# Seven half-size products in the second layer of the first two token blocks, one weight sum on VectorE, and a replanned order

## The chip, the cores and the metric

The kernel runs on one core of a Trainium2 chip. The core has a matrix engine (TensorE, PE in the profile; its weight loads are listed apart as PEld), a vector engine (VectorE, DVE), a scalar engine (ScalarE, ACT), GpSimd (POOL) and SyncE (SP), which here only issues transfers. Each engine works through its own list of instructions in order, and waits on semaphores where it needs what another engine makes. Matrix products are written to PSUM, eight banks of 128 partitions by 512 floats; everything else lies in SBUF or in device memory. The metric is the time of one execution on the device in microseconds (us). Less is better.

## The reference

Attention with a threshold, followed by a feed-forward layer, all in single precision:

```python
def _attn_ref(q, k, v, tau):            # (8, 8, 576, 64): batch, heads, positions, head size
    scores = scale * np.matmul(q, k.transpose(0, 1, 3, 2))
    thresh = np.max(scores, axis=-1, keepdims=True) - tau
    scores = np.where(scores >= thresh, scores, -1000000000.0)
    scores = scores - np.max(scores, axis=-1, keepdims=True)
    attn = np.exp(scores)
    attn = attn / (np.sum(attn, axis=-1, keepdims=True) + 1e-09)
    return np.matmul(attn, v).astype(np.float32)

def _moe_ref(x, w_in, w_out):           # x (4608, 512), w_in (512, 2048), w_out (2048, 512)
    h = x @ w_in
    g = h * (1.0 / (1.0 + np.exp(-1.702 * h)))
    return (g @ w_out).astype(np.float32)
```

The attention's result, with the heads of a position side by side, is the x of the second function. The two weight matrices come as 64-bit floats, and the kernel turns them into 32-bit ones itself.

## The kernel before

**Attention.** The 64 heads are worked as 32 pairs, numbered n, four pairs for each of the 8 batch entries. A pair's queries and keys are loaded and turned (`load_qk`, `turn_in`, `prep`), TensorE makes nine tiles of scores (`scores_run`, L598), ScalarE copies them out of PSUM (`keep`, L615), VectorE takes maxima (`in_groups`, L621), subtracts the threshold (`sub`, L695), ScalarE masks and exponentiates (`mask` L702, `exps` L706), VectorE sums, TensorE multiplies with the values (`values`, L717), and VectorE scales the result into the transposed x of the feed-forward layer (`place_x`, L821). For some pairs rows of maxima or sums go through device memory on GpSimd's queue (L671, L680, L686, L786, L793). From the seventh pair on, the values of one pair and the scores of a later one are interleaved on TensorE.

**Feed-forward.** The 4608 rows of x are 18 blocks of 256. A block can begin when all pairs of its batch entries are placed. Blocks 0 and 1 are worked together by `first_blocks` (L1543): the first layer (`mm1_0`, L895) makes 16 groups of 128 hidden columns for both blocks at once, ScalarE and VectorE apply the activation (`tanh` L851, `gelu_0` L901) into `g0`; the second layer (`mm2`, L864) multiplies, for each of four halves of 128 rows, 16 pieces of `g0` with the 16 pieces of `w_out`, 512 columns wide, and sums them in one PSUM bank; ScalarE halves the sum (`half`, L871) and SyncE stores it (`store_0`, L1426). A matmul in single precision is two instructions in the trace.

From block 2 on both layers use seven products of half size in place of eight (the scheme of Strassen and Winograd). For the second layer (`second` L2162, `product` L1399) a block's hidden values are four quarters a11, a12, a21, a22, and w_out four quarters. Seven products P1, P2, P6, P7, P4, P5, P3 are formed; three of them take sums of the block's quarters (`s_sums`, `s_minus`, `s_last`, L1017 to L1032, on VectorE), and four take sums t1 to t4 of weight quarters. Each product is 8 matmuls of 256 columns. `read` (L1404) adds the products into the output.

**The weight sums.** t1 to t4 are made once, after the second layer of the first two blocks, because they lie where `g0` lies or over w_out. For each, ScalarE writes one negated operand (`t_minus`, L1005), and a GpSimd transfer adds the other one to it in place (`t_plus`, L1009). Four like sums are made of w_in (`w_sums`, L930, L934).

**Weights.** w_in and w_out come in 16 pieces each. SyncE loads a piece to a staging place (`load_w`, L513), and five small steps on ScalarE and VectorE turn it to 32 bits (`cv_power` L521, `cv_power2` L525, `cv_low` L532, `cv_round` L539 or `cv_whole` L546, `cv_end` L553).

**The order.** While the program is built, each step is entered as a task with an engine, a cost, a rank, the tasks that it follows and the buffers that it takes and gives. `run_in_order` (L256) is a planner: it plays the tasks through with these costs, and an engine that is free takes the ready task of least rank. The instructions are issued in that order, and nothing reorders them on the chip. Feed-forward tasks of TensorE have the last rank, so that they fill the time between attention tasks. Ranks come from the pair's number plus constants in the tables `EARLY`, `SECOND`, `LATER`, `CV`, `W_RANK` and `L_RANK`. `FIRST` is ahead of all others.

## Time and profile before

| | us |
|---|---|
| median of 3 runs | 1241.7 |
| lowest and highest | 1241.35, 1242.64 |
| the profiled execution's own time | 1243.68 |
| its span in the profile | 1241.9 |
| TensorE busy | 1217.7 |
| VectorE busy | 1074.6 |
| ScalarE busy | 827.3 |

An execution's own time is a little longer than the span from its first to its last profiled instruction. A table of stretches gives, for each stretch, its length, then each engine's busy time with the number of instructions, the granted clock of TensorE, the share of the transfer engines and the rate. The chain that ended last goes back from the last instruction, at each step to what released it. A group of instructions has its busy time, the mean length of one in ns, and the idle time ahead of it with what ended that. A matmul's listed length holds its way through the array, so the distance between the starts of two is what one costs in a row.

### The profile page before, as it was taken

What the parts mean: (1) busy time and instruction counts of PE and PEld (TensorE: products, weight loads), DVE (VectorE), ACT (ScalarE), POOL (GpSimd) and SP (SyncE); (2) the same over time, 40 slices, a digit from 0 to 9 for tenths busy, and PEclk for the clock granted to TensorE, in tenths of its full rate; (3) what the DMA queues carried; (4) which work ended last, traced back from release to release, by engine and by line L of the source; (5) the groups of instructions that cost most, each with busy time, mean ns of one, the idle gap of its engine ahead of it and who ended that gap; (6) DMA issues with size and microseconds to landing.
All of it is one profiled execution on the core that took longest, in us unless ns stands there. A gap on an engine that the chain in (4) does not pass through costs nothing.

```text
span 1241.9 us, 26064 instructions
## 1 busy us (share of the span) xinstructions
PE 1217.7 (98%) x10592; PEld 980.9 (79%) x10592; DVE 1074.6 (87%) x1666; ACT 827.3 (67%) x1215; POOL 70.9 (6%) x115
## 2 busy tenths in 40 slices
PE   8889999999999999999999999999999999999998
PEld 5645854497888888888777777777887797999998
DVE  6988996779988988899689987998799889999797
ACT  7999978787665767585677467756875686430330
POOL 0111114110000000000100010000100000000000
PEclk9999999999999999999999999999999999999999
DMA  8846658793423132224423252224322432434443
GB/s 243 222 88 148 190 126 146 147 241 68 117 49 92 55 92 74 73 80 128 105 60 105 70 129 73 64 64 126 91 48 66 131 92 72 120 112 140 147 115 109
DMA packets 201512, 137.13 MB, mean 110 GB/s; under 512 B 146800, under 2 KB 163184, under 8 KB 201264
## 3 DMA queue, kind: packets, MB, share of 16 engines
q1 hardware_dynamic: 188992, 110.22, 33.1%
q0 software_dynamic: 11712, 24.95, 9.8%
q8 instruction: 83, 1.36, 0.5%
q10 hardware_dynamic: 688, 0.30, 0.1%
q14 instruction: 37, 0.30, 0.1%
HBM read 103.29 MB, written 23.75 MB: 102 GB/s over the span
## 4 chain that ended last, share of the span: by engine, by line
PE 85%; ACT 7%; DVE 5%; DMA 2%; issue 1%; SPq 0%; DVEq 0%; ACTq 0%
PE ops L1399 24%; PE pv L717 10%; PE ps L598 9%; PE hps L963 7%; PE hps L1105 7%; PE ps L963 5%; PE ps L1105 5%; PE ops L864 4%; PE ops L1360 4%; PE hps L1253 4%; PE ps L1360 3%; PE ps L1253 3%; ACT arena L706 2%; ACT arena L702 2%; ACT arena L615 2%; DMA w_out<-in_moe_w_in_dram 1%
## 5 line engine op out<-in xcount | busy, mean ns | idle before, releaser
L621 DVE TRANSPOSE_TENSOR_REDUCE part<-arena 128x36 f32<-128x1152 f32 x300 | 364.1, 1240 | 62.3 <-ACT arena L615 45.6
L615 ACT COPY arena<-ps 128x576 f32<-128x576 f32 x288 | 171.0, 641 | 102.8 <-PE ps L598 102.6
L702 ACT ACTIVATE arena<-arena 128x1152 f32<-128x1152 f32 (+1 forms) x160 | 164.5, 1059 | 54.4 <-DVE arena L695 54.3
L706 ACT ACTIVATE arena<-arena,shift,scl 128x1152 f32<-128x1152 f32 (+1 forms) x160 | 195.0, 1246 | 1.3
L695 DVE TENSOR_TENSOR arena<-arena 128x1152 f32<-128x1152 f32 (+1 forms) x150 | 180.4, 1242 | 0.7
L598 PE MATMUL ps<-arena 64*64 64x288 f32 x2304 | 171.8, 408 | 7.8 <-ACT arena L615 4.5
L1399 PE MATMUL ops<-w_out,arena 128*128 128x256 f32 x768 | 174.4, 381 | 0.0
L1399 PEld LDWEIGHTS ops<-w_out,arena 128*128 128x128 f32 x768 | 144.3, 190 | 24.9 <-issue 5.3
L717 PE MATMUL pv<-arena 64*64 64x288 f32 x2176 | 159.5, 405 | 0.0
L598 PEld LDWEIGHTS ps<-arena 64*64 64x64 f32 x2304 | 81.5, 132 | 70.9 <-ACT arena L615 27.2
L717 PEld LDWEIGHTS pv<-arena 64*64 64x64 f32 x2176 | 81.3, 133 | 53.1 <-issue 7.7
L1399 PE MATMUL ops<-arena 128*128 128x256 f32 x528 | 118.1, 379 | 0.0
L1399 PEld LDWEIGHTS ops<-arena 128*128 128x128 f32 x528 | 100.2, 190 | 14.0 <-issue 0.4
L640 ACT ACTIVATE other<-red,minus_gap 32x18 f32<-32x18 f32 x118 | 36.2, 307 | 34.3 <-DVE red L630 32.9
L1267 ACT COPY arena<-hps 128x512 f32<-128x512 f32 x38 | 22.2, 584 | 53.9 <-PE hps L1253 53.8
L864 PE MATMUL ops<-w_out,arena 128*128 128x512 f32 x128 | 55.9, 594 | 0.0
L1082 POOL DMA_DIRECT2D arena<-wrow x36 | 19.4, 540 | 602.8 <-PE ops L1399 484.0
L895 PE MATMUL hps<-xT,w_in 128*128 128x256 f32 x232 | 50.9, 380 | 1.3 <-DVE arena L901 1.3
L895 PEld LDWEIGHTS hps<-xT,w_in 128*128 128x128 f32 x232 | 43.7, 190 | 8.5 <-DVE arena L901 1.7
L864 PEld LDWEIGHTS ops<-w_out,arena 128*128 128x128 f32 x128 | 24.1, 190 | 30.1 <-issue 29.8
L1151 DVE TENSOR_TENSOR arena<-ps,arena 128x512 f32<-128x512 f32 x36 | 23.7, 686 | 26.1 <-PE ps L1105 26.1
L963 PEld LDWEIGHTS hps<-xT,w_in 128*128 128x128 f32 x384 | 44.2, 192 | 1.1 <-issue 0.9
(235 smaller groups left out, 1967.4 us busy)
## 6 DMA issues: line engine op xcount, KB each, us to landing
arena<-in_v_dram SPq DMA_DIRECT2D x128, 144.0 KB
arena<-exu SPq DMA_DIRECT2D x42, 256.0 KB
arena<-ext SPq DMA_DIRECT2D x39, 256.0 KB
arena<-wrow POOLq DMA_DIRECT2D x36, 256.0 KB, 3.0
out_dram<-osb SPq DMA_DIRECT2D x32, 256.0 KB
arena<-in_q_dram SPq DMA_DIRECT2D x112, 72.0 KB
arena<-in_k_dram SPq DMA_DIRECT2D x112, 72.0 KB
arena<-row_s SPq DMA_DIRECT2D x48, 144.0 KB
```

Of the source, the lines that this page charges most:

```text
L598: nc.tensor.matmul(ps[ts(c, KT), h, 0:SH], lhsT=mats[n, 1][ts(h, D), ts(j, KT)], rhs=mats[n, 0][ts(h, D), ts(c, SH)], start=True, stop=True,)
L615: nc.scalar.copy(out=sT[n, t][:, u], in_=pss.pop((n, j))[:, :, 0:SH])
L621: nc.vector.tensor_reduce(out=stats[n, op][:, t * 2 * QB : min(2 * t + 2, NK) * QB], in_=sT[n, t].rearrange("p u h (g d) -> p (u h g) d", ...
L695: engine.tensor_tensor(out=s, in0=s, in1=mbs[n].unsqueeze(1).to_broadcast(list(s.shape)), op=ALU.add if n in BY_DMA else ALU.subtract,)
L702: nc.scalar.activation(out=s, in_=s, func=AF.Prelu, alpha=STEEP)
L706: nc.scalar.activation(out=s, in_=s, func=AF.Exp, scale=scl, bias=shift)
L717: nc.tensor.matmul(o[c][ts(h, D), 0:SH], lhsT=left(j, h)[ts(c, KT)], rhs=sT[n, t][ts(c, KT), u, h, :], start=(j == 0), stop=(j == NK - 1),)
L864: nc.tensor.matmul(acc[i], lhsT=g0[:, j, ts(i, P)], rhs=w_out[:, j, :], start=(j == 0), stop=(j == NFC - 1),)
L895: nc.tensor.matmul(hidden[j][:, ts(i, BLK)], lhsT=w_in[:, c, ts(j, P)], rhs=xTs[i][:, c, :], start=(c == 0), stop=(c == NDC - 1), skip_gro ...
L963: nc.tensor.matmul(o[:, ts(j, HT)], lhsT=left[:, c, ts(4 * y + j, P)], rhs=right[:, c, :], start=(x in (P1, P2, P5) and j + c == 0), stop= ...
L1105: nc.tensor.matmul(o[:, ts(j, BLK)], lhsT=left[:, c, ts(j, P)], rhs=right[:, c, :], start=(x in (P1, P2, P5) and j + c == 0), stop=(j + c ...
L1399: nc.tensor.matmul(banks[blk][k][:, ts(o, HM)], lhsT=left[:, j, :], rhs=right[:, j, :], start=(j == 0), stop=(j == HF - 1),)
```

## The change

The second layer of blocks 0 and 1 also goes by seven products a block. `g0` is laid out by quarters: half of the hidden columns, block, group, row. The order of the products of a block is P1, P2, P5, P6, P7, P3, and P4 of both blocks comes at the end, since t4 is written where a quarter of block 0 lay. A block uses three PSUM banks one after the other, and a product waits until what lies in its bank is read. The first weight sum t1 is made by two subtractions on VectorE after the last piece of w_out; t2 and t3 by ScalarE and GpSimd after it; t4 after P7 of block 0. VectorE's sums of the hidden values and the output of block 0 lie in spare x buffers. The later blocks use the same four weight sums.

The planner's costs of the first loads, of the first ScalarE instruction and of the first matmuls are new, and so are all constants in the rank tables, which change the order of the whole program. The core of the diff:

```diff
     EARLY = {
-        "add_row": -0.11,
+        "add_row": 9.44,
...
     CV = {
-        "cv_end": 102.19,
-        "cv_low": 7.35,
-        "cv_power": 316.63,
-        "cv_power2": 317.96,
+        "cv_end": -2.47,
+        "cv_low": -12.63,
+        "cv_power": 46.33,
+        "cv_power2": -0.05,
...
-    def mm2(i, part):
-
-        if part == 0:
-            acc[i] = psM.tile([P, d_model], FP32, name="ops", tag="mo")
-        for j in range(2 * part, 2 * part + 2):
-            nc.tensor.matmul(
-                acc[i], lhsT=g0[:, j, ts(i, P)], rhs=w_out[:, j, :],
-                start=(j == 0), stop=(j == NFC - 1),
-            )
...
+    def t_first(k):
+        o, a, b = (y[:, ts(k, HF // 2), :] for y in T_SUMS[0])
+        nc.vector.tensor_tensor(out=o, in0=a, in1=b, op=ALU.subtract)
...
+    FIRSTS = {
+        P1: (0, 0), P2: (1, 0), P5: (0, 1), P6: (1, 1), P7: (0, 0), P3: (1, 0), P4: (2, 0),
+    }
+
+    def product_0(blk, x, js):
+        left, right = PRODUCTS[x][:2]
+        left = quarters(blk)[left[0]][left[1]] if isinstance(left, tuple) else s_homes(blk)[x != P5]
+        k, o = FIRSTS[x]
+        if x in (P1, P2, P4) and js[0] == 0:
+            banks[blk, k] = psM.tile([P, BANK], FP32, name="ops", tag="mo")
+        for j in range(*js):
+            nc.tensor.matmul(
+                banks[blk, k][:, ts(o, HM)], lhsT=left[:, j, :], rhs=right[:, j, :],
+                start=(j == 0), stop=(j == HF - 1),
+            )
+
+    def read_0(blk, x):
...
+        if x == P1:
+            nc.scalar.activation(out=c21, in_=ps, func=AF.Copy, scale=FACTOR[0])
+        sums = {
+            P1: (), P2: [(c11, c21)], P5: [(c12, c21)], P6: [(c12, c12), (c21, c21)],
+            P7: [(c22, c12), (c21, c21)], P3: [(c12, c12)], P4: [(c21, c21)],
+        }
+        for e, a in sums[x]:
+            nc.vector.scalar_tensor_tensor(
+                out=e, in0=ps, scalar=FACTOR[0], in1=a, op0=ALU.mult, op1=ALU.add
+            )
...
-    W_RANK = (-44.98, 0.18, -1.8, 76.35, 1.62, -16.84)
+    W_RANK = (-138.99, 6.52, -4.17, 189.65, 11.68, 9.31)
...
-    warm = task("ACT", 1.5, -2.0, first_act)
-    warmth = [task("PE", 3.6, -20.0, run_up, take=("psM",), give=("psM",))]
+    warm = task("ACT", 2.3, -2.0, first_act)
+    warmth = [task("PE", 4.4, -20.0, run_up, take=("psM",), give=("psM",))]
...
-        for x in range(4):
-            after = t_ready[-1:] + (ffn[-1:] if x > 1 else []) + ready_w[n_in:]
+
+        def t_sum(x, after):
             for k in range(2):
                 after = [task("ACT", 1.0, T_RANK, t_minus, x, k, after=after)]
             a = task("POOL", 1.6, T_RANK, t_plus, x, after=after)
-            t_ready.append(transfer("DMW", 6.5, a, 1, lag=2.0))
+            return transfer("DMW", 6.5, a, 1, lag=2.0)
+
+        firsts = [task("DVE", 1.15, T_RANK, t_first, k, after=ready_w[n_in:]) for k in range(2)]
+        t_of = {P5: firsts, P6: [t_sum(1, firsts)], P7: [t_sum(3, firsts)]}
...
+            one(blk, P1, gs[0])
+            one(blk, P2, gs[1])
+            one(blk, P5, [[a] for a in sums])
+            one(blk, P6, [[a] for a in sums])
+            lasts = [task("DVE", 0.6, FIRST, s_last, blk, k, after=ffn[-1:]) for k in range(2)]
+            one(blk, P7, [[a] for a in minus])
+            one(blk, P3, [[a] for a in lasts])
+            if blk == 0:
+                t_of[P4] = [t_sum(2, t_of[P6] + [used[0, P7]])]
+        for blk in range(PLAIN):
+            one(blk, P4, gs[1])
+            for i in range(2):
+                task(
+                    "SP", 0.6, FIRST, store_0, blk, i,
+                    after=[y for (z, _), y in reads.items() if z == blk],
+                    give=("osb",) if blk else ("xT",) if i else (), lag=2.2,
+                )
...
-            cost, moves, ring = (0.6, 0.6, RING[0]) if which else (1.2, 0.72, RING[3])
+            cost, moves, ring = (0.6, 0.6, RING[0]) if which else (2.3 if n in (1, 3) else 1.2, 0.72, RING[3])
...
-        lv = task("SP", 2.45, r + (1.85 if n < 2 else -1.2) + load_rank(n, 2), load_v, n, after=lvs[-1:], take=(v_m,) + RING[2])
+        lv = task("SP", 3.8 if n < 2 else 2.45, r + (1.85 if n < 2 else -1.2) + load_rank(n, 2), load_v, n, after=lvs[-1:], take=(v_m,) + RING[2])
```

More of the change, by code (lines that the diff above doesn't have):

```diff
@@ new lines, in first_blocks @@
+        for blk in range(PLAIN):
+            before = ffn[-1:]
+            gs = [[[gelus[HF * f + 4 * y + z] for z in range(4)] for y in range(2)] for f in range(2)]
+            sums = []
+            for y in range(2):
+                sums.append(task(
+                    "DVE", 1.33, FIRST, s_sums, blk, y, after=before + gs[0][y] + gs[1][y] + sums[:1],
+                    take=("xT",) * 2 if y + blk == 0 else (),
+                ))
+            minus = [task("DVE", 0.6, FIRST, s_minus, blk, y, after=[sums[y]]) for y in range(2)]
+            one(blk, P1, gs[0])
[7 more added lines that the diff above has]
+                t_of[P4] = [t_sum(2, t_of[P6] + [used[0, P7]])]
@@ L2259, in two_loads @@
             a = task(
-                "SP", 0.05 if apart else cost, r, load_qk, n, which, queue if apart else nc.sync, h,
+                "SP", 0.05 if apart else cost + (0.7 if which and not n else 0.0), r, load_qk, n, which, queue if apart else nc.sync, h,
                 after=behind + ([a] if h else []), take=((),  tuple(take))[not h] + (() if apart else ring),
             )
-            ys.append(transfer("DMS", moves, a, lag=1.5 if n else 2.0, give=() if apart else ring))
+            ys.append(transfer("DMS", moves, a, lag=2.0, give=() if apart else ring))
         return ys
```

235 lines of the change are left out of this document (137 added, 98 removed).

## The prediction

> **What bounds the kernel now.** I read the page's busy shares first, then a table of stretches that I cut where the first two blocks begin and end, then the chain that ended last, in order of time.
>
> ```profile
> PE 1217.7 (98%) x10592; PEld 980.9 (79%) x10592; DVE 1074.6 (87%) x1666; ACT 827.3 (67%) x1215; POOL 70.9 (6%) x115
> ...
> 0.00:113.00 113.00, 97.97 (x1413) 61.63 (x1416) 89.52 (x137) 103.36 (x147) 19.39 (x39) 1.00 0.68 166
> 113.00:175.40 62.40, 60.07 (x384) 48.85 (x377) 61.13 (x98) 56.53 (x87) 8.20 (x12) 1.00 0.71 191
> 175.40:253.60 78.20, 78.20 (x491) 37.54 (x490) 55.80 (x75) 58.98 (x77) 20.75 (x26) 1.00 0.74 137
> 253.60:1055.00 801.40, 801.40 (x6733) 655.45 (x6735) 705.25 (x1006) 558.76 (x809) 22.55 (x38) 1.00 0.36 91
> 1055.00:1242.00 187.00, 180.07 (x1588) 177.45 (x1580) 162.87 (x355) 49.63 (x98) 0.00 (x0) 0.99 0.41 124
> ```
>
> The columns after a stretch and its length are the busy times of TensorE, its weight loads, VectorE, ScalarE and GpSimd, then the granted clock (full everywhere), the DMA share and rate. TensorE is busy in all of the 801.4 us from 253.6 to 1055. So whatever starts at 253.6, the first product of block 2, sets the end: the end moves by as much as that start moves. Before it TensorE is idle 15.0 us up to 113 and 2.3 us up to 175.4, and not at all from there to 253.6, where the second layer of the first two blocks lies. A saving of TensorE work there is worth its full size only if nothing else makes TensorE wait in its place.
>
> ```profile
> 166.92 8.83 PE hps L895 x40
> 175.75 20.60 PE ops L864 x48
> 196.35 4.53 PE pv L717 x72
> 200.88 10.50 PE ops L864 x24
> 220.34 22.51 PE ops L864 x52
> 251.82 1.92 PE ops L864 x4
> 253.73 3.57 PE hps L963 x32
> ...
> 252.92 0.91 DVE L821 TENSOR_TENSOR xT<-pv,arena 128x192 f32<-128x192 f32 x4
> ```
>
> Each row of the chain gives its start and its length. The first layer ends at 175.7, the old second layer fills TensorE between the attention's slots, and block 2 follows its last piece at 253.7. The last row, from VectorE's work in order of time, is the thing to notice: it places the last attention pair that block 2 needs from 252.92 to 253.83. Filler and attention end together, so neither alone decides.
>
> **TensorE's work removed and added.**
>
> ```profile
> L864 PE MATMUL ops<-w_out,arena 128*128 128x512 f32 x128 | 55.9, 594 | 0.0
> L864 PEld LDWEIGHTS ops<-w_out,arena 128*128 128x128 f32 x128 | 24.1, 190 | 30.1 <-issue 29.8 <-PE ops L864 0.2
> L1399 PEld LDWEIGHTS ops<-w_out,arena 128*128 128x128 f32 x768 | 144.3, 190 | 24.9 <-issue 5.3 <-DVE red L777 0.9
> ...
> 357.11 20.92 PE ops L1399 x96
> ```
>
> Removed are 128 instructions (64 matmuls of two each) of 512 columns. Their four pieces on the chain above take 20.60 + 10.50 + 22.51 + 1.92 = 55.5 us, 0.434 each. Added are two blocks of seven products of eight matmuls, 224 instructions of 256 columns. The later blocks run just these: 96 in a row take 20.92 us on the chain, 0.218 us each, so 48.8 us. **TensorE saves 6.7 us.** The 96 additional weight loads cost nothing, because a load of 190 ns lies beside a 218 ns product; 96 in 20.92 us leave no place for it elsewhere.
>
> The Trainium skill (TensorE: Matmul & The Clock Gate, Part 3) says that a weight load overlaps a running matmul only if it goes to another row group; these loads fill all rows. By that rule the added loads would stand in the open and the sum would end on the slower side (rival 4); the row of 96 does not agree.
>
> **VectorE's work.** The change adds per block eight additions or subtractions of 128x512 (four in s_sums, two in s_minus, two in s_last) and eight reads of a 128x256 product.
>
> ```profile
> L1021 DVE TENSOR_TENSOR arena<-arena x24: 681/685/693, 283.0 to 1023.6; 128x512 f32<-128x512 f32 x24
> L1421 DVE SCALAR_TENSOR_TENSOR osb<-ops,osb 128x256 f32<-128x256 f32 x84 | 33.7, 413 | 7.4 <-PE ops L1399 7.1
> 245.75 1.38 DVE L621 TRANSPOSE_TENSOR_REDUCE part<-arena 128x36 f32<-128x1152 f32 x1 [1.75 <-ACT arena L615]
> ...
> 251.62 1.38 DVE L621 TRANSPOSE_TENSOR_REDUCE part<-arena 128x36 f32<-128x1152 f32 x1 [0.32 <-ACT arena L615]
> 281.86 1.20 PE L717 MATMUL pv<-arena 64*64 64x288 f32 x16
> ```
>
> That is 8 x 0.685 + 8 x 0.413 = 8.8 us a block, 17.6 for two; the first weight sum adds two subtractions of 128x1024, at twice the 512-wide one 2.7 us. In all 20.3 us. VectorE has 1.3 us idle from 113 to 175.4 and 22.4 us from 175.4 to 253.6, 23.7 together. With TensorE's saving taken out of the stretch, 17.0 remain for 20.3: 3.3 us too few. But four of its reductions there (the first and the last are shown, 1.38 each, 5.5 in all) belong to the pair whose values TensorE takes only at 281.9, and can wait. So the cost lies between 0 and 3.3 us; I take 0, because the rows of those reductions are what stands last in the stretch, and keep 3.3 for the range. If this cover is gone, each added operation pushes the subtractions of the last pair, and block 2 starts late.
>
> **The weight sums, the new wait.** The old products of an input half need only the w_out rows that they use. The new third product (P5) needs the first sum of all w_out rows, the fourth (P6) a sum that ScalarE negates and a GpSimd transfer adds, the fifth (P7) another.
>
> ```profile
> 183.85 0.69 DVE L553 SCALAR_TENSOR_TENSOR w_out<-arena,w_out 128x512 int32<-128x512 int32 x1
> ...
> 185.27 1.98 ACT L1005 ACTIVATE arena<-w_out 128x1024 f32<-128x1024 f32 x2
> 189.47 3.06 POOL L1009 DMA_DIRECT2D arena<-w_out  x1
> ...
> DMA to landing us min/median/max: 10.0/12.4/13.4
> ```
>
> In the old order the last w_out rows stand at 184.5. From there: the first sum 2.7, ScalarE's negation 2.0 (as in the second row), the transfer 12.4 from issue to landing, so 201.6. P6 would be due when P1, P2 and P5 are through: 48 instructions of 0.218 after 175.7, at 186.2. That is 15.4 us of wait, of which the attention slot at 196.35 fills 4.5: **10.9 us** if the order stayed (P2's own wait for the last rows lies inside it). The lower end is nothing, if the new order converts w_out 15.4 us sooner. The order is new in every rank and the planner that makes it has this wait in its model, but prices the transfer at 1.6 + 6.5 + 2.0 = 10.1 us, in the added lines. The row says 12.4, so an order that is just in time by the plan is 2.3 us late on the chip. I take 2.3, the value nearest to that row, and keep 0 and 10.9. Behind the waiting P6 stand all later filler products on TensorE; attention slots that are already ahead of it in the order fill part of the wait. On GpSimd's queue the two early transfers now stand among the rows of the running pairs (the third row is queued right behind such rows): a row behind a transfer that waits for ScalarE would hold its pair. No price for that is in the trace; it is inside the 10.9.
>
> **Moved for nothing.** ScalarE loses four half-scalings and one negation and gains two reads. The four output stores, as many and as large as before, now come at the end of both blocks, and block 0's result stays in a spare x buffer until then.
>
> ```profile
> L871 ACT ACTIVATE osb<-ops 128x512 f32<-128x512 f32 x4 | 2.3, 584 | 2.5 <-PE ops L864 2.5
> L1414 ACT ACTIVATE osb<-ops 128x256 f32<-128x256 f32 x12 | 4.5, 374 | 5.0 <-PE ops L1399 5.0
> ...
> SPq L1426 <- ACT osb L871: 29.9, 3, 17.0
> ...
> 29.18 7.71 SPq L471 DMA_DIRECT2D arena<-in_v_dram  x8
> ```
>
> ScalarE gets 2.3 + 2.0 - 0.75 = 3.6 us freer; it is not what ends last in this stretch (59.0 busy of 78.2), so I count nothing. A store holds SyncE's queue until its data are there (17.0 us once), and the loads of later pairs stand behind it; the next values are taken at 281.9, 28 us after the stretch, which hides this. Each later product waits until the earlier one in its PSUM bank is read: 0.4 to 0.8 us of reading, behind at most one 1.38 us reduction, inside the 3.5 us of the product between. That cover goes if VectorE's queue stands behind something late.
>
> **The opening.** The planner's prices of first loads are new; the last row shows why: eight value loads took 7.71 us, 3.86 a pair, where the old price was 2.45 and the new is 3.8. For two pairs the old plan was 2.8 us short on SyncE's queue. TensorE's 15.0 us of idle time up to 113 can shrink or grow by about as much with a new order; what the order is cannot be read from the trace. Minus 2.8 to plus 2.8, taken as 0, as nothing shows a side.
>
> **The sum:** -6.7 (products) + 2.3 (P6's wait) + 0 (VectorE) + 0 (opening) = -4.4 us. The profiled execution took 1243.7 us, 1.8 of it around its span of 1241.9, so its like would take 1239.3. The median of the runs is 2.0 lower, 1241.7, so I predict **1237.3**.
>
> **The rivals.**
> 1. The weight sums come late (slower). For it: w_out stands 15.4 us too late in the old order, and VectorE, which converts it, has 1.3 us free in the stretch where it would have to be done sooner. Against: the attention there has slack to be put behind, and the plan knows the need. It decides from a wait of 6.7 us, that is when w_out stands less than 4.2 us sooner against the end of the first layer than now. At 10.9 us of wait: 1241.7 - 6.7 + 10.9 = 1245.9; with VectorE's 3.3 on top 1249.2.
> 2. The saving turns into idle time (no change). For it: the last pair is placed at 253.83 now, and VectorE's ledger is 3.3 us over. If the placing doesn't move, TensorE waits 6.7 us before block 2 and the time stays 1241.7. Against: ScalarE and VectorE have 19.2 and 22.4 us idle in that stretch, so the pairs there wait for each other's steps and not for room.
> 3. The new order also helps the opening: P6 in time and 2.8 us won, 1241.7 - 6.7 - 2.8 = 1232.2. For it: the 15.0 us of idle time; against: ScalarE is busy 103.4 of the 113 us, and that is work, not order.
> 4. Weight loads in the open: 96 more of 0.190 us, 18.2 us, would give 1241.7 - 6.7 + 18.2 = 1253.2. The row of 96 in 20.92 us is against it. The Trainium skill's page TensorE: Matmul & The Clock Gate (Part 3) is what speaks for it.
>
> **How the numbers follow.** Forecast 0.52; rival 1 0.27; rival 2 0.11; rival 3 0.09; rival 4 0.01. The bound between a change and none is 0.2%, 2.5 us, about what a measurement of this kernel can tell: 1239.2 and 1244.2. Forecast and rival 3 are faster, 0.61; rival 2 is the same, 0.11; rivals 1 and 4 are slower, 0.28. The forecast's own range is 1234 to 1239. The whole range goes down to 1231, a little under rival 3, and up to 1247, past 10.9 us of wait; what lies above, VectorE's 3.3 on top and rival 4, and what lies below are less than 2 in 10.
>
> **What would show it.** Right: the second layer of the first two blocks as 224 matmul instructions of 256 columns, 0.218 us apart, 48.8 us; block 2's first product near 249, and 801 us without idle time after it. P6 of block 0 waits about 2 us for the GpSimd transfer, which lands some 12 us after its issue. VectorE's part up to block 2 is 20 us larger. Wrong: P6 or P7 waits 7 us or more (rival 1); TensorE stands for VectorE's placing just before block 2 (rival 2); the first layer ends clearly sooner than 175 (rival 3) or, the side that I cannot exclude, later, because w_out is converted ahead of the attention; distances of 0.4 us between the added products (rival 4). The tail after 1055, with 6.9 us idle and all its ranks new, could move by some us of its own; I count nothing for it.

## The result, and the profile after

| | before | after |
|---|---|---|
| median of the runs (us) | 1242.06 | 1254.12 |
| lowest and highest | 1241.35, 1242.64 | 1253.43, 1255.84 |
| the profiled execution's own time | 1243.68 | 1255.84 |
| its span | 1241.9 | 1254.1 |

The runs of both kernels in this table, four of each, were made side by side (the 1241.7 that the prediction starts from is the median of three of them). The ratio is 1.0098, with a 95% interval of 1.0086 to 1.0110: the changed kernel is 12.1 us slower, where 4.4 us faster was predicted.

The same stretches as in the prediction's table, cut in the changed kernel where the first layer begins (127.9), where it ends (189.4) and where block 2 begins (261); the columns are as before:

```profile
0.00:113.00 113.00, 91.76 (x1272) 57.60 (x1276) 91.53 (x137) 103.70 (x146) 13.73 (x31) 0.94 0.69 183
113.00:127.90 14.90, 13.08 (x152) 7.07 (x144) 12.59 (x24) 14.49 (x24) 5.88 (x8) 1.00 0.77 143
127.90:189.40 61.50, 60.13 (x381) 48.99 (x378) 58.53 (x87) 56.30 (x78) 12.58 (x16) 1.00 0.73 164
189.40:261.00 71.60, 71.55 (x586) 55.59 (x585) 61.93 (x98) 46.47 (x63) 18.03 (x23) 1.00 0.69 128
261.00:1062.00 801.00, 797.80 (x6674) 652.37 (x6673) 695.25 (x993) 552.82 (x798) 19.39 (x36) 1.00 0.34 87
1062.00:1254.00 192.00, 182.83 (x1641) 178.76 (x1639) 169.67 (x364) 55.36 (x107) 0.00 (x0) 1.00 0.42 125
```

Three differences make up the 12.2 us of the spans. The second layer of blocks 0 and 1 takes 71.6 us in place of 78.2, **6.6 less**, and TensorE is busy in all of it. What lies ahead of it ends at 189.4 in place of 175.4, **14.0 more**. And from block 2's start to the end it is 993.1 in place of 988.3, **4.8 more**, because TensorE now has 3.2 us of idle time between 261 and 1062 (none before) and 9.2 after that (6.9 before). -6.6 + 14.0 + 4.8 = 12.2. (Taken from the starts of the first products themselves, 175.59 and 253.57 before, 189.39 and 260.99 after, the first two are 6.4 less and 13.8 more; the cut at 175.4 lies 0.2 us early.) By the list of TensorE's waits after block 2's start, 3.0 us of the longer rest are waits of scores for ScalarE's copies (L615), which the kernel before does not have there, and 4.4 us in place of 2.4 are waits of the last blocks' first layer for VectorE.

The products themselves, from TensorE's work in order of time (start, length), the first and the last of blocks 0 and 1 and the start of block 2:

```profile
189.39 7.07 PE L1401 MATMUL ops<-w_out,arena 128*128 128x256 f32 x32
196.29 1.89 PE L1401 MATMUL ops<-arena,xT 128*128 128x256 f32 x8
...
255.71 5.45 PE L1401 MATMUL ops<-arena 128*128 128x256 f32 x24
260.99 1.28 PE L949 MATMUL hps<-xT,w_in 128*128 128x128 f32 x10
```

The first 32 start at 189.39 and the next instruction at 196.29: 0.216 us each. No row of these products has idle time ahead of it. The weight sums were there in time. VectorE's last conversion step of w_out and its two subtractions for the first sum, in order of time:

```profile
170.12 0.69 DVE L553 SCALAR_TENSOR_TENSOR w_out<-arena,w_out 128x512 int32<-128x512 int32 x1
170.72 2.35 DVE L999 TENSOR_TENSOR arena<-w_out 128x1024 f32<-128x1024 f32 x2
```

w_out stands at 170.8, 18.6 us ahead of the end of the first layer; in the kernel before it stood 9 us behind that end. What went ahead of the first layer for this shows in the next rows: ScalarE's groups of the two power steps (L521 and L525) up to the start of the first layer, first in the kernel before (up to 113.4; the rounding steps, L539, are 16 in both kernels and left out):

```profile
L525 ACT ACTIVATE w_in<-w_in,rebias 128x512 int32<-128x512 f32 x9 | 6.6, 729 | 0.2
L521 ACT ACTIVATE w_in<-w_out,rebias 128x512 f32<-128x512 int16 x8 | 6.2, 776 | 0.6 <-DMA w_out<-in_moe_w_in_dram 0.6
...
L521 ACT ACTIVATE w_in<-arena,rebias 128x512 f32<-128x512 int16 x2 | 1.5, 764 | 0.0
```

and in the changed kernel (up to 127.93):

```profile
L525 ACT ACTIVATE w_in<-w_in,rebias 128x512 int32<-128x512 f32 x16 | 11.6, 727 | 0.4
L521 ACT ACTIVATE w_in<-w_out,rebias 128x512 f32<-128x512 int16 x12 | 9.3, 777 | 4.5 <-DMA w_out<-in_moe_w_in_dram 4.5
...
L521 ACT ACTIVATE w_in<-arena,rebias 128x512 f32<-128x512 int16 x4 | 3.2, 795 | 0.0
...
L525 ACT ACTIVATE w_out<-w_out,rebias 128x512 int32<-128x512 f32 x4 | 2.9, 722 | 0.1
L521 ACT ACTIVATE w_out<-w_out,rebias 128x512 f32<-128x512 int16 x2 | 1.6, 776 | 0.0
L521 ACT ACTIVATE w_out<-arena,rebias 128x512 f32<-128x512 int16 x2 | 1.5, 752 | 0.0
```

40 steps with 30.1 us stand where 19 with 14.3 stood: 15.8 us more on ScalarE, which had 103.4 us of work in the first 113. VectorE's conversion steps up to the same points are 13.7 us more. These rows say what was added, not yet that it costs the 14 us; that is for the experiments.

Where the 14 us show at the end of the opening can be read from the last pair of batch 0. Its last exponential, its last value product, its placing and the start of the first layer in the kernel before, rows of three engines in order of time:

```profile
106.14 0.87 ACT L706 ACTIVATE arena<-arena,shift,scl 128x576 f32<-128x576 f32 x1
108.73 0.66 PE L717 MATMUL pv<-arena 64*64 64x288 f32 x8
110.64 0.95 DVE L821 TENSOR_TENSOR xT<-pv,arena 128x256 f32<-128x256 f32 x4
113.35 1.99 PE L895 MATMUL hps<-xT,w_in 128*128 128x256 f32 x8
```

and the same in the changed kernel, with what stands on VectorE between the turning of the sums (L804) and the placing:

```profile
108.38 4.58 ACT L706 ACTIVATE arena<-arena,shift,scl 128x1152 f32<-128x1152 f32 x4
117.91 0.67 PE L717 MATMUL pv<-arena 64*64 64x288 f32 x8
120.68 0.78 DVE L804 STREAM_TRANSPOSE arena<-r 128x576 f32<-128x576 f32 x1
121.38 0.65 DVE L553 SCALAR_TENSOR_TENSOR w_out<-w_out 128x512 int32<-128x512 int32 x1
...
125.32 1.38 DVE L621 TRANSPOSE_TENSOR_REDUCE part<-arena 128x36 f32<-128x1152 f32 x1
126.62 0.91 DVE L821 TENSOR_TENSOR xT<-pv,arena 128x256 f32<-128x256 f32 x4
127.93 1.99 PE L881 MATMUL hps<-xT,w_in 128*128 128x256 f32 x8
```

The exponentials end at 107.0 and 113.0 (6.0 later), the value products 2.4 and 5.6 us after them (3.2 more), the placing 2.2 and 8.9 us after those (6.7 more, with conversion steps of w_out and a later pair's reductions in the queue), and the first layer starts 1.8 and 0.4 us after that (1.4 less): 6.0 + 3.2 + 6.7 - 1.4 = 14.5. The first layer itself is then 0.8 us shorter.

Last, TensorE's ledger up to the first product of block 2, before and after (the first pair of numbers behind the length is TensorE's busy time and its instructions; the granted clock is the third number from the end):

```profile
0.00:253.73 253.73, 236.37 (x2282) 148.15 (x2283) 206.58 (x308) 218.87 (x308) 48.34 (x77) 1.00 0.71 163
```

```profile
0.00:260.99 260.99, 236.51 (x2376) 169.24 (x2377) 224.57 (x344) 220.95 (x309) 50.22 (x78) 0.97 0.70 161
```

The idle time went from 17.4 to 24.5 us. The busy time is the same although the products save 6.7: the rest of the instructions, the same in number (the counts differ by the 96 that the products add, but for two), took that much longer, at a granted clock of 0.94 in the first 113 us. So on TensorE's own ledger the loss is about half idle time and half slower work.

### The profile page after: what moved, and what is told of

The parts are those of the page before. It is cut to its first block, busy times and chain, and to the rows that moved or that the text cites. A ratio compares the mean times of both kernels' runs of the same rounds, so it can differ in the third digit from the quotient of the medians.

```text
span 1254.1 us, 26284 instructions
## 1 busy us (share of the span) xinstructions
PE 1217.2 (97%) x10688; PEld 1000.4 (80%) x10688; DVE 1089.5 (87%) x1700; ACT 829.1 (66%) x1213; POOL 69.6 (6%) x114
## 4 chain that ended last, share of the span: by engine, by line
PE 79%; ACT 11%; DVE 4%; DMA 3%; issue 2%; SPq 0%; POOL 0%; DVEq 0%; ACTq 0%; POOLq 0%
PE ops L1440 23%; PE pv L717 10%; PE ps L598 9%; PE hps L949 6%; PE ps L949 5%; PE hps L1106 5%; PE ops L1361 4%; PE ops L1401 4%; PE ps L1106 3%; PE hps L1254 3%; PE ps L1361 3%; ACT arena L706 3%; ACT arena L702 3%; PE ps L1254 2%; PE hps L881 2%; ACT arena L615 2%
## 5 line engine op out<-in xcount | busy, mean ns | idle before, releaser
L621 DVE TRANSPOSE_TENSOR_REDUCE part<-arena 128x36 f32<-128x1152 f32 (+1 forms) x300 | 365.5, 1242 | 59.1 <-ACT arena L615 44.7
L615 ACT COPY arena<-ps 128x576 f32<-128x576 f32 x288 | 171.2, 643 | 95.1 <-PE ps L598 94.6
L1440 PEld LDWEIGHTS ops<-w_out,arena 128*128 128x128 f32 x768 | 144.1, 190 | 25.7 <-issue 7.0
L1440 PEld LDWEIGHTS ops<-arena 128*128 128x128 f32 x528 | 100.2, 190 | 14.4 <-DVE part L621 0.4
L881 PE MATMUL hps<-xT,w_in 128*128 128x256 f32 x232 | 51.1, 381 | 1.3 <-DVE arena L887 1.3
L949 PE MATMUL hps<-xT,w_in 128*128 128x128 f32 x384 | 45.0, 275 | 0.0
L1106 PE MATMUL hps<-xT,w_in 128*128 128x256 f32 x192 | 43.9, 380 | 0.0
```

The costliest lines, as they stand in the source:

```text
L615: nc.scalar.copy(out=sT[n, t][:, u], in_=pss.pop((n, j))[:, :, 0:SH])
L621: nc.vector.tensor_reduce(out=stats[n, op][:, t * 2 * QB : min(2 * t + 2, NK) * QB], in_=sT[n, t].rearrange("p u h (g d) -> p (u h g) d", ...
L881: nc.tensor.matmul(hidden[j][:, ts(i, BLK)], lhsT=w_in[:, c, ts(j, P)], rhs=xTs[i][:, c, :], start=(c == 0), stop=(c == NDC - 1), skip_gro ...
L949: nc.tensor.matmul(o[:, ts(j, HT)], lhsT=left[:, c, ts(4 * y + j, P)], rhs=right[:, c, :], start=(x in (P1, P2, P5) and j + c == 0), stop= ...
L1106: nc.tensor.matmul(o[:, ts(j, BLK)], lhsT=left[:, c, ts(j, P)], rhs=right[:, c, :], start=(x in (P1, P2, P5) and j + c == 0), stop=(j + c ...
L1440: nc.tensor.matmul(banks[blk][k][:, ts(o, HM)], lhsT=left[:, j, :], rhs=right[:, j, :], start=(j == 0), stop=(j == HF - 1),)
```

## The experiments

**The order or the products.** e1 keeps the old products and takes over all of the new order; e2 does the opposite.

```diff
# e1, against the kernel before (e2: the same lines the other way round, against the changed kernel)
     EARLY = {
-        "add_row": -0.11,
+        "add_row": 9.44,
...
     CV = {
-        "cv_end": 102.19,
+        "cv_end": -2.47,
...
-    warm = task("ACT", 1.5, -2.0, first_act)
+    warm = task("ACT", 2.3, -2.0, first_act)
```

> The products of before with all rank tables and planner prices of after. Theory (the order of the opening costs the time: 20 weight pieces in place of 9 are finished ahead of the first layer, on a ScalarE that is busy anyway): the first layer starts near 128 us as in after (113.4 in before), the second layer takes its old 78 us, and the total is 1254 + 6.7 = 1261 us, between 1255 and 1266. Rival (the new products and VectorE's added sums cost the time, the order is harmless): the first layer starts at 113 to 116 us and the total is 1240 to 1244 us.

> The products of after with all rank tables and planner prices of before. Theory: the opening is that of before, the first layer starts at 113.4 and ends near 175.5 us, but w_out is then finished near or after 184 us and the second layer waits: for the weight sums 10.9 us at least, and for the last pairs, which VectorE's added work pushes. Block 2 starts at 258 to 270 us in place of 253.6 (261 in after) and the total is 1246 to 1262 us; so the early conversions of after were bought for these sums. Rival (the order of after is merely bad): block 2 starts near 247 us and the total is 1235 to 1238 us.

e1: 1262.58 us, ratio 1.0162 (1.0146 to 1.0177). The first layer starts at 125.8, 12.4 us later than in the kernel before, and the rest from block 2 on is 993.9. So the late opening and the longer rest come with the order, and with the old products too. The new products are worth about 8 us there (1.0162 against 1.0098).

e2: 1273.93 us, 1.0249 (1.0234 to 1.0264), beyond what was expected. The opening is nearly back: the second layer starts at 177.0. But now w_out and the weight sums are late. VectorE's rows of the last conversion and the first sum, GpSimd's row of the transfer for the second sum, and rows of TensorE (attention values, the second half of P2 and the product that needs the second sum), each in order of time; last, the ledger up to block 2:

```profile
196.73 0.69 DVE L553 SCALAR_TENSOR_TENSOR w_out<-arena,w_out 128x512 int32<-128x512 int32 x1
197.33 2.36 DVE L999 TENSOR_TENSOR arena<-w_out 128x1024 f32<-128x1024 f32 x2
...
201.79 1.66 POOL L995 DMA_DIRECT2D arena<-w_out  x1
...
189.47 2.20 PE L717 MATMUL pv<-arena 64*64 64x288 f32 x16 [7.15 <-ACT arena L706]
...
199.50 1.99 PE L1401 MATMUL ops<-w_out,arena 128*128 128x256 f32 x8
...
212.65 5.34 PE L1401 MATMUL ops<-arena,xT 128*128 128x256 f32 x16 [7.70 <-ACT arena L706]
...
0.00:270.69 270.69, 237.40 (x2377) 168.75 (x2377) 225.51 (x342) 221.17 (x313) 49.76 (x78) 0.95 0.72 161
```

w_out stands at 197.4, 12.9 us later than in the kernel before. TensorE has P1 and half of P2 to do, then waits 8.3 us in all for the exponentials of the attention values that come next in its queue, and does the other half of P2 from 199.5, once the last rows of w_out stand. At P6 it waits another 7.7 us, until 10.9 us after the transfer was issued (ScalarE's exponentials, named there, were the last to signal; the product uses the transfer's sum and not them). It has 33.3 us idle up to block 2, 15.9 more than in the kernel before. The rest from block 2 on is 1001.4, 13.1 more than in the kernel before, 11.3 of it in one wait of the last blocks' first layer (L1254, up to 1097.6 us) for VectorE (L1226). So the new products need w_out early: at block 2's start, with the products' saving already taken off, the old order is 17.1 us behind the kernel before (270.7 against 253.6) and the new order 7.4 (261.0). Which part of the new order costs the opening these two runs cannot say, since all ranks change at once.

**The first sum.** e3 makes the first sum as the kernel before made all of them, by ScalarE and a GpSimd transfer.

```diff
-        firsts = [task("DVE", 1.15, T_RANK, t_first, k, after=ready_w[n_in:]) for k in range(2)]
+        firsts = [t_sum(0, ready_w[n_in:])]
```

> After, with the first weight sum by two ScalarE copies and a GpSimd transfer as in before, everything else as in after. Theory: the opening stays (first layer from 128 us), the first sum lands 2.1 + 12 us after the last piece in place of 2.4, so t2 and t3 land 12 us later, at about 201 and 204 us where P6 was due at 203: P5 is due at 196 and its sum lands near 185, so TensorE waits little in the old timing, and the total is 1254 to 1262 us. Rival (the weight sums are the end of the chain in after): the total is 1264 to 1268 us.

1268.69 us, 1.0206 (1.0189 to 1.0223). The first layer starts at 126.6, the second at 192.3, block 2 at 267.6. The rest from block 2 on is 999.2. VectorE's first sum is not the loss; without it the kernel is slower still (1.0206 against 1.0098). That is above both forecasts, and no product of the second layer waits for a sum. As the planner also moved a pair, this is no clean price of the sum.

**The conversion work.** e4 adds work to the kernel before, e5 takes work from the changed one.

```diff
# e4
-        nc.scalar.activation(out=o, in_=top, func=AF.Prelu, bias=rebias, alpha=2.0**-40)
+        for _ in range(2 if i < 10 else 1):
+            nc.scalar.activation(out=o, in_=top, func=AF.Prelu, bias=rebias, alpha=2.0**-40)
# e5
-        nc.scalar.activation(out=o, in_=top, func=AF.Prelu, bias=rebias, alpha=2.0**-40)
+        nc.scalar.activation(
+            out=o, in_=top, func=AF.Prelu, bias=rebias, alpha=2.0**-40, scale=0.0 if i < 20 else 1.0
+        )
...
     def cv_power2(i):
         o = cv[i][3]
+        if i < 20:
+            return
```

> Before, with the first of the two power steps of the first ten weight pieces done twice on ScalarE, ten instructions of 0.74 us more ahead of the first layer and no other difference in any engine's order. Theory (an us of ScalarE ahead of the first layer costs an us of the total): first layer and total 5 to 7.5 us later, 1247 to 1250 us. Rival (slack in the order hides it): less than 2 us, 1241 to 1244 us.

> After, with the second power step left out for the 20 weight pieces that it finishes ahead of the first layer, and the first power step of the same pieces multiplied by nothing, so that the weights are not the real ones: 20 ScalarE instructions of 0.72 us, 14.5 us, less, and every engine's order as in after. Theory (ScalarE's conversions ahead of batch entry 0's attention set the start of the first layer): the first layer starts 9 to 14 us sooner, at 114 to 119 us in place of 128, and the total is 1241 to 1246 us. Rival (the start is set by the order of VectorE or by the attention's own waits): less than 4 us sooner, 1250 to 1254 us.

e4: 1249.38 us, 1.0049 (1.0034 to 1.0064): 7.4 us of additional ScalarE work moved the first layer from 113.4 to 120.4, block 2 by 7.1 to 260.7, and the time by 6.1 (0.49%). In the kernel before ScalarE has no room ahead of the first layer for such steps. e5: 1253.56 us, 1.0094 (1.0077 to 1.0110). With 14.4 us of ScalarE's work gone, the first layer started only 5 us sooner (122.9), block 2 at 257.4, and the ratio hardly moved (1.0098 to 1.0094). The ledger of e5 up to block 2:

```profile
0.00:257.42 257.42, 233.59 (x2377) 168.75 (x2378) 223.99 (x344) 208.53 (x289) 50.02 (x78) 0.99 0.71 163
```

ScalarE's idle time up to there grew from 40.0 to 48.9 us. Of the 3.6 us that were won there, 2.9 are TensorE's busy time (236.5 to 233.6), at a granted clock of 0.98 in place of 0.94 up to 113 us. The theory that ScalarE's additional work alone holds the opening fell here: adding work to the kernel before cost its length, but taking it out of the finished order did not give it back.

**The clock.** e6 gives the fillers that keep TensorE busy (`stay_warm`, L1506) nine matmuls in place of four.

> After, with nine small matmuls in place of four in each of the 22 idle fillers of TensorE in the opening, same order. In after the granted clock is 0.77 to 0.89 between 40 and 80 us, in before 1.00. Theory (ScalarE bounds the opening): the clock may recover, the total stays within 2 us of 1254. Rival (the lower clock costs the opening its time): the clock is 1.00 from 40 to 80 us and the total is 1247 to 1251 us.

1263.16 us, 1.0170 (1.0154 to 1.0185), neither of the two forecasts. The granted clock was 1.00 from 40 to 70, but the first layer started at 134.7, 6.7 us later. The ledger up to block 2:

```profile
0.00:268.42 268.42, 246.74 (x2597) 181.38 (x2598) 226.03 (x348) 220.96 (x309) 50.22 (x78) 0.99 0.68 158
```

The added matmuls are themselves 10.2 us of TensorE's work (236.5 to 246.7), in the queue of the attention, so this run does not part the price of the low clock from the price of the fillers. What e5 says of it is a bound: with the clock at 0.98 and 14.4 us less work on ScalarE, the first layer still started 9.6 us later than in the kernel before. The low clock is not the whole of the loss; its share is not shown.

**Both engines, and the start.** e7 leaves out VectorE's steps too, e8 moves up pair 0's first loads, e9 does both.

```diff
# e7 (with e5's edit)
     def cv_low(i):
+        if 10 <= i < 20:
+            return
# ... the same in cv_round, cv_whole and cv_end
# e8
     def run_in_order():
+        for which in (1, 0):
+            load_qk(0, which, nc.scalar, 0)
+            load_qk(0, which, nc.sync, 1)
# ... and load_qk returns where a load has been issued already
```

> The changed kernel with the conversion work ahead of the first layer cut back to about what the kernel before has there, on both engines, while all loads and the order stay: for the first 20 pieces of w_in ScalarE's second step is left out (and its first step works with a scale of 0), and for pieces 10 to 19 all steps on VectorE and the rounding on ScalarE are left out too, so w_in is wrong for these pieces. ScalarE loses about 14.4 us and the rounding steps of ten pieces, VectorE about 13.7 us. Theory A (the work that both engines have to do ahead of the last pair of batch 0 holds the opening): the first layer starts at 113 to 117 in place of 127.9, block 2 begins at 246 to 251, time 1239 to 1246; what is left above the kernel before is the loss after block 2's start. Theory B (not the work, but the order: late first loads and steps that wait in turn): the first layer starts at 121 to 125, block 2 at 255 to 259, time 1250 to 1255, as in the run that left out ScalarE's share alone.

> The changed kernel with the loads of the first pair's queries and keys issued ahead of everything else, four transfers on ScalarE's queue and four on SyncE's, as early as in the kernel before; all other work in the order that it has. Nothing is left out. The changed kernel has its first scores at 13.9 us, the kernel before at 8.1. Theory A (the work holds the opening): the scores begin near 9, but VectorE and ScalarE have the same work to do up to the first layer, and it starts at 125 to 129, time 1251 to 1256. Theory B (late first loads): the 5.5 us are won, the first layer starts at 120 to 124, block 2 at 253 to 257, time 1246 to 1251.

> Both edits of the last two runs: conversion work ahead of the first layer cut back on both engines (w_in wrong for 20 pieces), and the first pair's loads at once. If the work alone holds the opening: as the run with the work cut back, 1239 to 1246. If both do: the first layer starts at 109 to 114, block 2 at 241 to 248, time 1234 to 1241, that is the 6.7 us of the products become visible. If neither: 1249 or more.

e7: 1254.37 us, 1.0095 (1.0073 to 1.0116); first layer at 125.9, 3.0 us later than in e5 although more work was left out, at a granted clock of 0.88 in place of 0.98 up to 113 us. So the start in a single profiled execution may carry some us that go with the clock. e8: 1257.76, 1.0121 (1.0104 to 1.0139); 128.7. e9: 1254.99, 1.0097 (1.0071 to 1.0123); 129.3. e8 and e9 were aimed badly: the new order begins with pair 1, so pair 0's loads went ahead of the ones that were needed first, and the first scores came at 16.5 in place of 13.9. e10 moves pair 1's loads instead (and one half of pair 0's, on ScalarE's queue), and keeps e7's edit:

```diff
+        for n, queue in ((1, nc.sync), (0, nc.scalar)):
+            for which in (1, 0):
+                for h in range(2 if n else 1):
+                    load_qk(n, which, queue, h)
...
+        if name.startswith("cv_") and a[0] < 4 and "maxima" not in state:
+            waiting.append((f, a))
+            return
# ... a step that waits follows behind a later copy, reduction or activation step
```

> The order of the changed kernel begins with pair 1, and the run before last moved up the loads of pair 0, ahead of pair 1's, so it did not test the start. Here the queries and keys of pair 1 are loaded ahead of the first weight pieces, and the conversion steps of the first four pieces come after the first maxima, one behind each later copy or reduction; and the conversion work is cut back on both engines as in e7_both_engines_work_as_before (w_in wrong for 20 pieces). Theory C (late start and conversion work each hide the other: whichever is taken away alone, the other still holds the last pair of batch 0): first scores near 9 in place of 13.9, the first layer starts at 113 to 119, time 1239 to 1247. Theory D (neither; the order of the later steps alone, such as copies between the exponentials and the late placing): the first layer starts at 122 or later, time 1249 to 1255, as without the start moved.

1254.38 us, 1.0088 (1.0073 to 1.0103). The first scores came at 10.5, the first layer at 126.3, block 2 at 258.6. So neither the work of both engines nor the start, nor the two together, is what a single edit can give back. Two views of e10 show one reason, TensorE's last values of batch 0 in order of time, and a table of stretches around them:

```profile
104.18 0.72 PE L637 MATMUL ps<-arena 64*64 64x288 f32 x8 [1.02 <-DVE xT L860]
107.44 2.20 PE L756 MATMUL den<-arena,ones 64*64 64x288 f32 x16 [2.54 <-ACT arena L745]
109.41 2.14 PE L756 MATMUL pv<-arena,arena 64*64 64x288 f32 x16
...
115.39 1.14 PE L756 MATMUL pv<-arena,arena 64*64 64x288 f32 x16
...
100.00:107.40 7.40, 3.88 (x62) 1.92 (x52) 6.32 (x15) 5.07 (x6) 0.00 (x0) 0.89 0.81 199
107.40:112.90 5.50, 5.46 (x48) 2.93 (x52) 1.29 (x3) 4.83 (x7) 0.00 (x0) 0.52 0.59 94
112.90:118.00 5.10, 5.10 (x85) 2.81 (x77) 1.06 (x5) 2.50 (x5) 3.04 (x6) 1.00 0.23 50
```

ScalarE has 2.3 of 7.4 us idle there, because its masks wait for rows that come through device memory; then the four exponentials stand together behind the masks, and TensorE, which waited for the first of them, does the values at half its clock. In this place the work left out turned into waits.

**The steps ahead of the first layer.** e11 places the last pair at once and puts w_out's steps behind the start of the first layer; e12 adds the early start.

```diff
+        if name == "place_x" and a[0] == 3:
+            return
+        if name.startswith("cv_") and a[0] >= n_in and "sums" in state and "first" not in state:
+            waiting.append((f, a))
+            return
         f(*a)
...
+        if name == "spread_sums" and a[0] == 3:
+            place_x(3)
# ... once the first layer has begun, each follows behind a later copy, reduction or activation step
```

> The changed kernel, complete, with one thing moved: the last pair of batch 0 is placed right after its sums are ready on VectorE, and the w_out conversion steps that stand in the queues of ScalarE and VectorE between that pair's last value product and the start of the first layer (4 pieces: 8 steps of 0.74 us on ScalarE, 4 of 0.66 on VectorE) follow after the first layer has started. In the changed kernel TensorE ends that pair's values at 118.6 and starts the first layer at 127.9, with copies of scores behind conversion steps in between; in the kernel before it was 109.4 and 113.4. If these steps cost what they take: the first layer starts at 122 to 125, the time falls by 3 to 6, to 1248 to 1251, and w_out, finished 18.6 us ahead of the first layer's end, is still in time for the weight sums. If other work fills the place: 1252 or more.

> The same with the early start of e10_start_and_work_as_before, again complete: pair 1's loads ahead of the weight pieces, the conversion steps of the first four pieces behind the first maxima. If the late start costs its 5 us on top: the first layer starts at 117 to 121, time 1243 to 1247. If ScalarE's and VectorE's work up to there decides, the steps that are put off are paid later: within 1.5 us of e11_steps_behind_last_pair.

e11: 1259.95 us, 1.0132 (1.0116 to 1.0148). e12: 1261.61, 1.0149 (1.0132 to 1.0166). The placing of e11 and its first products in order of time:

```profile
120.83 0.95 DVE L849 TENSOR_TENSOR xT<-pv,arena 128x256 f32<-128x256 f32 x4
...
125.70 1.99 PE L909 MATMUL hps<-xT,w_in 128*128 128x256 f32 x8
133.14 3.35 PE L909 MATMUL hps<-xT,w_in 128*128 128x256 f32 x7 [5.44 <-DVE arena L915]
```

The pair was placed 5.8 us sooner and the first layer began 2.2 us sooner. Then TensorE waited 5.4 us: the conversion steps now stood in front of the first layer's own tanh and products on ScalarE and VectorE, and its end came 4.3 us later than in the changed kernel (193.7). In either place something waits behind these steps. The early start of e12 gained 0.9 us at that place, and nothing in the time.

**Pair 2's tiles.** In the kernel before, eight score tiles of pair 2 are copied ahead of pair 0's exponentials; in the changed kernel they stand between them, as pair 2's loads come some 15 us later. e13 moves them there in the kernel before. e14 (on e10) and e15 (on the changed kernel) move them, and the loads, the other way.

```diff
# e13
+        sc, kp, gr = at("scores_run", 2)[:8], at("keep", 2), at("in_groups", 2)
+        ex = at("exps", 0)
+        move(sc[0:3] + kp[0:3], ex[1])
+        move(sc[3:6] + gr[0:1] + kp[3:6], ex[2])
+        move(sc[6:8] + gr[1:3] + kp[6:8] + gr[3:4], ex[3])
# e14, e15
+        move(at("load_qk", 2), at("load_qk", 0)[3])
...
+        move([y for k in range(8) for y in (sc[k], kp[k])] + gr[:4], at("over_halves", 0)[0], True)
```

> The kernel before, complete, with only the place of pair 2's first eight score tiles changed: their products, copies (8 of 0.6 us on ScalarE) and four reductions (1.38 us each on VectorE) follow behind the second, third and fourth exponential of pair 0, where the changed kernel has them, in place of ahead of the first. Conversion steps, loads and all else stay. If this order holds the opening: pair 0 is placed 4 to 7 us later (62 to 65 in place of 58.0), the first layer starts at 117 to 121 in place of 113.4, time 1246 to 1251. If the engines only trade idle time for it: within 2.5 us of 1242.

> The kernel of e10_start_and_work_as_before (conversion work cut on both engines, w_in wrong for 20 pieces, and the start moved up) with the opposite move: pair 2's loads right behind pair 0's on SyncE's queue, its turns behind the other pairs' turns, and its first eight score tiles, their copies and four reductions ahead of pair 0's maxima, as in the kernel before. If the place of these steps is what still held the opening: the first layer starts at 114 to 120 in place of 126.3, time 1241 to 1248. If not: 124 or later, 1251 or more.

> The complete changed kernel with the same move of pair 2's loads, scores, copies and reductions. The conversion steps stay where they are, ahead. If work and order act together, the steps moved forward now push pair 0's exponentials by their own 5 us, and little is won: the first layer starts at 124 to 129, time 1250 to 1257. If the order alone matters: 118 to 122, 1245 to 1249.

e13: 1244.28 us, 1.0014 (1.0005 to 1.0024). The first layer starts 1.8 us later (115.2), block 2 1.8 later. So this part of the order is worth about 2 us in the kernel before. e14: 1264.73, 1.0182 (1.0165 to 1.0200). e15: 1266.39, 1.0190 (1.0173 to 1.0207). These two went wrong in the queue: pairs 0 and 2 share a buffer for their rows, so pair 2's loads had to wait for pair 0's, and everything behind them on SyncE waited too. (In both, pair 0 is computed from pair 2's rows.) SyncE's queue in e14:

```profile
12.02 8.76 SPq L495 DMA_DIRECT2D arena<-in_k_dram  x3
```

Three loads held the queue for 8.8 us, and pair 0 was placed at 79.4. They say nothing on the question.

**What stays open.** Shown: the late opening comes with the new order and does not need the new products (e1: 12.4 of the 14.6 us at the first layer's start), the order is what brings w_out early, and the old order with the new products is worse (e2). The rows show 15.8 us more conversion work ahead of the first layer, and e4 shows that such work, added to the kernel before, costs its length. Not shown is how the 14 us divide over the order's parts and the lower clock: no part, taken back in the finished order, returned more than 5 us at the first layer. That another step was then the late one is seen in e10 and e11; for the rest it is an argument. No kernel here beats the kernel before.

## Why the prediction failed, point by point

- **TensorE's work, -6.7 us: right.** The stretch is 6.6 shorter, 0.216 us an instruction, no idle time. Rival 4 (weight loads in the open) fell with it: a load of 190 ns still lies beside each product. That its 1253.2 is near the median of 1254.1 is chance.
- **VectorE, 20.3 us for nothing: right for its place.** VectorE's busy time up to block 2 rose by 18.0 (206.58 to 224.57). TensorE has no wait in the second layer.
- **The weight sums, 2.3 us: 0 measured.** The lower end came true, but the argument for that end was incomplete: "nothing, if the new order converts w_out 15.4 us sooner" has no price for the sooner conversion. The order moved w_out forward by 27.6 us against the first layer's end (9 behind to 18.6 ahead), and the work that this displaced was charged nowhere. It was also more than the sums needed: the transfer for P6 was issued at 174.99, so by the 12.4 us of the prediction's row it was down near 187, and P6 of block 0 starts near 204 (an estimate, from P5's 16 instructions ending there). By this about 17 us were to spare; no run keeps the new order and converts w_out that much later.
- **The opening, "minus 2.8 to plus 2.8, taken as 0": the step that failed.** It measured +14.0. The bounds came from the late loads alone, the one thing that the prediction read there; ScalarE, 103.4 busy of 113, is named only against rival 3. In its place the runs showed that the new order makes the opening late with either products (e1: 12.4 us at the first layer's start). It puts 15.8 us more of conversion steps on that full engine, and e4 gives the price of such steps in the kernel before: 7.4 us of them, 7.1 us lost at block 2. That they make up all of the 14.0 is not shown (e5, e7). The last part of the prediction names this side ("later, because w_out is converted ahead of the attention") and gives it neither price nor chance.
- **The tail, "I count nothing": +4.8.** With the old products it goes with the rank tables: 993.9 with the new order (e1), 986.9 to 988.3 with the old one (the kernel before, e4, e13). With the new products the old tables are no better: 1001.4 in e2. So "the end moves by as much as that start moves" held in e4 and e13 (within 1.4 us), where the program's order stayed but for the edit, and not where the planner made a new one.
- **The rivals.** Rival 1 had the sign, but by late sums, which did not occur. Its mechanism is what e2 shows, and there its price was too low: 7.7 us of wait at the product that needs the second sum, and 8.3 at the attention values while P2's rows were missing, 16.0 together, where 10.9 had been given with P2's wait "inside it". Rival 2 and rival 3 did not occur.

With the measured terms the sum is 1241.7 - 6.6 + 14.0 + 4.8 = 1253.9; the median is 1254.1.

## What to carry to other kernels

When a change needs a result sooner, the price is the work that has to go ahead of it on the engines that make it: count those steps, and look at how full these engines are in the stretch where the steps must go, not in the stretch where they were. A wait and the early work that avoids it are two ends of one bill: here block 2 started 17.1 us late with the one and 7.4 with the other, both with the saving of the products already taken off. And in queues that run in turn, work that was added cost its length at once (7.4 us added, 7.1 lost), while 14.4 us taken out of the finished order gave back 3.6 at the same place.

## What the runs showed of the hardware

Short waits of TensorE were followed by half the clock. In e10, after a stretch with 3.88 us busy of 7.40 (its last wait 2.54 us), the granted clock was 0.52 for the next 5.5 us, and 16 instructions took 2.20 us in place of 1.14 (rows above). The Trainium skill (TensorE: Matmul & The Clock Gate, Part 1) puts the fall after an idle window of about 3.4 us; here no single wait was that long: waits of 1.02 and 2.54 us with 0.72 us of work between them came ahead of it. Nine matmuls in place of four in each filler held the clock at 1.00 from 40 to 70 us and made the kernel about 9 us slower (e6).
